# Four transfers for the key weight rows, two of them on ScalarE's queue, and a first tile scaled in halves

## The chip, the cores and the metric

The kernel runs on one core of one Trainium2 chip. The metric is device time in microseconds (us) of one execution; smaller is better. Before the change, three runs took 563.38, 563.44 and 564.0 us; their median is 563.44.

## The reference, cut to what matters

```python
xn = layernorm(x)                                  # x: 2048 x 512
q, k, v = split(xn @ wqkv)                         # 32 heads of 16
pq, pk = q @ w_phi, k @ w_phi                      # per head, 16 x 16
phi = concat(softmax(p), softmax(-p))              # for p = pq and p = pk
kv, z = phi_k^T v, sum(phi_k)                      # per head
s = ((phi_q kv) / (phi_q z + 1e-6)) @ wo
g = silu((relu(xn @ W_gate) * (xn @ W_up)) @ W_down)
out = x + s * g
```

All inputs are float32. Each large product is made of three products of float32r operands, a high and a low part (`mm3`, line 198).

## The kernel before

The 2048 rows of x are 16 tiles of 128 rows. For each tile n the kernel normalizes the rows, transposes the tile on TensorE (`transpose_x`, line 297), and projects it to keys and values (`project`, line 358), and later to queries. The gate, up and down products follow, for 11 chunks f of 128 hidden columns, and last the output product. TensorE has work in every stage.

The key and query weights are not used as they come. `fold(w, raw, k)` (line 243) multiplies row block k of the transposed weight with a block-diagonal matrix made of `w_phi` (the tile `cb`): four float32 products of 128x128 into one PSUM bank, each recorded as two passes. ScalarE and VectorE then split the result into high and low parts (`split`, line 193; tiles `wkh` and `wkl`). So the folds of the key weight need `cb` and the rows of `wkT`; the first key product `pk` needs the folds and the transposed first tile.

What happens first, by the program (lines 950 to 1018):

- Lines 953 to 966 issue loads, nearly all on SP's queue: x tile 0; the identity (`ident`) on ScalarE's queue; `cb`; row blocks 0 and 1 of `wkT` in one transfer of 512 KB; row block 2; row block 3 (256 KB each); x tile 1; then query rows, value rows and more x tiles.
- Lines 968 to 972: VectorE clears a tile `idle`, and TensorE multiplies it with itself twelve times (24 passes, `pidle`). Nothing reads these products. Line 973 fills `mhalf`, the exponent -0.5 that the norm needs.
- Lines 983 to 993: `norm_vector(0)` (line 278) takes mean and variance on VectorE and the power on GpSimd; `norm_vector_apply(0)` (line 288) scales the tile in one VectorE instruction; `turn(0, False)` (line 319) transposes it in four 128x128 steps and copies the high part to `XT`. Then come the folds of row blocks 0 and 1, then of 2 and 3.
- Line 995: `pk`, the first key product, then the folds of the query weight, and for the value weight the high parts on ScalarE (`wv_hi`) and the low parts on GpSimd (`wv_lo`, tile `wvl`).
- The value product of tile 0, `pv`, reads `wvl`.

The order of each engine's instructions is the order in which the program writes them: every call goes through `InOrder` (line 45). For later stages the program decides when to write a piece of side work by a planner, `Clock` (line 62). It adds up an estimate for each engine, takes 8000 of its units for a DMA to land (line 69), and lets a piece of work go when its inputs are due (`due`, line 121). `pump` (line 134) is called between products.

The weights of the hidden chunks f = 2 and f = 3 (`AHEAD`, line 36) are loaded first, during the early tiles, by `f_load` (line 455): for each f two transfers of 256 KB into the halves of one tile `rawg` and one into `rawd`. `all_preps` (line 1020) then waits 30 steps of 512 planner units before `f_prep` uses them.

Of the kernel before, what the change touches and what calls it, by code (L numbers as in the profile page):

```python
# [9 lines left out]
AF = mybir.ActivationFunctionType  # L10
ALU = mybir.AluOpType
AX = mybir.AxisListType

P = 128
S = 2048
D = 512
# [3 lines left out]
KD = D // P  # L20
# [15 lines left out]
AHEAD = (2, 3)  # L36
# [122 lines left out]
def layer_kernel(ctx: ExitStack, tc: tile.TileContext, x, wkT, wqT, wv, wo, wf, cst, out):  # L159
    pace = Clock()  # L160
    nc = InOrder(tc, pace)
# [4 lines left out]
    def ps(shape=(P, 512), name="ps"):  # L166
        return pp.tile(list(shape), F32, tag="ps", name=name)

    def u8(shape, name, dt=F32):
        return sb.tile(list(shape), dt, tag="u8", bufs=B8, name=name)  # L170

    def u4(shape, name, dt=F32):
        return sb.tile(list(shape), dt, tag="u4", bufs=B4, name=name)

    def u2(shape, name, dt=F32):
        return sb.tile(list(shape), dt, tag="u2", bufs=B2, name=name)

    def small(n, name, bufs=3):
        return sb.tile([P, n], F32, tag=name, bufs=bufs, name=name)
# [43 lines left out]
    def load_x(n):  # L223
        b, i = order[n]
        t = b * TPB + i
        X[n] = u2((P, D), "xt")
        nc.sync.dma_start(X[n], x[t * P:(t + 1) * P, :])
# [26 lines left out]
    mhalf = sb.tile([P, 96], F32, name="mhalf")[:, 0:1]  # L254
# [32 lines left out]

    def norm_vector_apply(n):
        xn, xt, mv, rs = XN[n]
        nc.vector.tensor_scalar(xn, xt, mv[:, 0:1], rs, op0=ALU.subtract, op1=ALU.mult)  # L290
        XN[n] = xn

    def cols(n):
# [151 lines left out]
    RAW, FT, WD = {}, {}, {}  # L445

    def two(name, apart):
        if apart:
            return [u2((P, 2, 2, P), name) for c in range(2)]
        t = u4((P, 2, 2, 2, P), name)  # L450
        return [t[:, c] for c in range(2)]
# [1 line left out]
    DONE = set()  # L453

    def f_load(f):
        RAW[f] = two("rawg", f not in AHEAD), u2((P, D), "rawd")
        for c in range(2):
            nc.sync.dma_start(RAW[f][0][c].rearrange("p k s f -> p (k s f)"), wf[f][:, c * 512:(c + 1) * 512])
        nc.sync.dma_start(RAW[f][1], wf[f][:, 1024:])

    def w_pair(name):
# [10 lines left out]
    def f_prep(f, keep=True):  # L472
# [47 lines left out]
        if keep:  # L520
            FT[f], WD[f] = [wa, wb, wc, wd], fd
            nxt = f + 1
            while nxt in AHEAD:
                nxt += 1
            del rg, rd, ta, tb
            if nxt < NF:
                f_load(nxt)
# [422 lines left out]
    wk_raw, wv_raw, wq_raw = u8((P, KD, D), "wkT"), u8((P, KD, D), "wvr"), u8((P, KD, D), "wqT")  # L950
    bd_sb = u2((P, KD, P), "cb")
    ident = sb.tile([P, P], F32, name="ident")
    load_x(0)
    nc.scalar.dma_start(ident, cst[:, KD, :])
    nc.sync.dma_start(bd_sb, cst[:, :KD, :])
    nc.sync.dma_start(wk_raw[:, 0:2, :], wkT[:, 0:2, :])
    nc.sync.dma_start(wk_raw[:, 2, :], wkT[:, 2, :])
    nc.sync.dma_start(wk_raw[:, 3, :], wkT[:, 3, :])
    load_x(1)
    nc.sync.dma_start(wq_raw[:, 0:2, :], wqT[:, 0:2, :])  # L960
    nc.sync.dma_start(wv_raw[:, 0:2, :], wv[:, 0:2, :])
# [3 lines left out]
    for n in range(3, 7):  # L965
        load_x(n)

    idle = u2((P, P), "idle")
    nc.vector.memset(idle, 0.0)
    p = ps((P, P), name="pidle")  # L970
    for _ in range(12):
        nc.tensor.matmul(p, idle, idle, start=True, stop=True)
    nc.vector.memset(mhalf, -0.5)
    zacc = u4((P, H, 2, DH), "zacc")

    WK, WV, WQ = w_tile("wk"), w_tile("wv"), w_tile("wq")
# [4 lines left out]
    def wv_lo(k):  # L981
        add(nc.gpsimd, by_parity(WV[k][1]), even_first(wv_raw[:, k, :]), f32(by_parity(WV[k][0])), ALU.subtract)
    norm_vector(0)
    norm_vector_apply(0)
    px = turn(0, False)
    folds = [fold(WK, wk_raw[:, k, :], k) for k in range(2)]
# [5 lines left out]
    norm_vector(1)  # L992
    folds[1]()
    norm_vector_apply(1)
    pk = project(0, WK, "pk")
    folds = [fold(WQ, wq_raw[:, k, :], k) for k in range(2)]
# [14 lines left out]
    for s in range(2):  # L1011
        exp_part(early, s)
    norm_vector(3)
    norm_vector_apply(2)
    sums_x(1)
    folds[0]()
# [3 lines left out]
    def all_preps():  # L1020
        for f in AHEAD:
            f_load(f)
            yield 30,
            yield from f_prep(f, False)
        f_load(0)
        yield 30,
        for f in range(NF):
            if f not in AHEAD:
                while at[0] < (START[f] if f < 2 else N + f - 1):
                    yield 3,  # L1030
                if f in WO_WITH:
                    wo_fetch(WO_WITH.index(f))
                yield from f_prep(f)
                if f in WO_WITH:
                    yield from wo_prep(WO_WITH.index(f))
# [289 lines left out]
```

## Time and profile before

| quantity | value |
|---|---|
| median of three runs | 563.44 us |
| profiled execution, own time | 564.6 us |
| its span, from the first to the last instruction | 562.8 us |
| mean granted TensorE clock in the span | 0.998 |
| TensorE products busy | 555.9 us, 99% |
| VectorE, ScalarE, GpSimd busy | 412.4, 282.3, 416.7 us |
| DMA | 137.98 MB, mean 245 GB/s |

The profile is of one execution. The own time of that execution holds 1.8 us beside its span. In rows of a timeline the columns are start, duration (both us), engine, source line, operation, the tile written, the tiles read, the shapes and the count; in brackets stands how long the engine was idle before it and what released it. Nearly all rows have line 58, since all instructions go through one helper, so one goes by the names of tiles. PE is TensorE's products, PEld its weight loads, DVE VectorE, ACT ScalarE, POOL GpSimd, SP the SyncE queue; ACTq and SPq are the issues of DMAs. A row of waits gives the waiting engine and its tile, what it waited for, the us in total, how many times, and the longest. Consecutive products overlap in the records.

### The profile page before, as it was taken

The numbers are of one execution on the slowest core, as the hardware profiler recorded it, in microseconds if no ns is written. First come the engines' busy times: TensorE is split into PE (matmuls) and PEld (weight loads), VectorE is DVE, ScalarE is ACT, GpSimd is POOL, SyncE is SP. The second block draws the span as 40 slices with busy tenths as digits, with TensorE's granted clock in tenths as the row PEclk, the third lists the DMA queues.
The fourth block names the chain that finished last, engine by engine and source line by source line (L and its number), as shares of the span: only waits on it lengthen the run. The fifth ranks groups of instructions, "written<-read, shape, count | busy, mean of one in ns | idle before, by whom it ended". The sixth has DMA issues, their size and how long they took to land.

```text
span 562.8 us, 8204 instructions
## 1 busy us (share of the span) xinstructions
PE 555.9 (99%) x2620; PEld 465.1 (83%) x2620; DVE 412.4 (73%) x621; ACT 282.3 (50%) x504; POOL 416.7 (74%) x356
## 2 busy tenths in 40 slices
PE   8999999999999999999999999999999999999996
PEld 7888888888888888888888888888888888888885
DVE  4978866677656898999797432799995959684224
ACT  3898787675555446444425251234563644535500
POOL 1689987999888386998889242573779888888375
PEclk9999999999999999999999999999999999999999
DMA  8349999856599828979867999997485766669684
GB/s 294 122 137 257 260 278 292 243 162 188 149 295 314 325 77 278 321 276 315 289 219 230 252 364 418 397 380 272 119 244 169 219 192 206 206 200 263 165 236 183
DMA packets 84538, 137.98 MB, mean 245 GB/s; under 512 B 7824, under 2 KB 34320, under 8 KB 83600
## 3 DMA queue, kind: packets, MB, share of 16 engines
q1 hardware_dynamic: 81040, 125.33, 65.4%
q0 software_dynamic: 3312, 12.06, 11.1%
q8 instruction: 21, 0.34, 0.2%
q14 instruction: 21, 0.17, 0.1%
q10 hardware_dynamic: 144, 0.07, 0.0%
HBM read 76.87 MB, written 52.69 MB: 230 GB/s over the span
## 4 chain that ended last, share of the span: by engine, by line
PE 97%; DMA 1%; DVE 1%; issue 0%; SPq 0%; DVEq 0%
PE py L58 21%; PE pc L58 11%; PE pd L58 11%; PE pa L58 11%; PE pv L58 8%; PE pk L58 8%; PE pq L58 8%; PE pso L58 7%; PE pb L58 5%; PE pkv L58 3%; PE pnum L58 3%; PE pfold L58 1%; PE pxT L58 1%; DMA wkT<-wkT 1%; DVE yk L58 1%
## 5 line engine op out<-in xcount | busy, mean ns | idle before, releaser
L58 PE MATMUL py<-fdh,hh 128*128 128x512 f32 x176 | 68.5, 389 | 0.0
L58 PE MATMUL py<-fdh,hl 128*128 128x512 f32 x176 | 68.5, 389 | 0.0
L58 PE MATMUL py<-fdl,hh 128*128 128x512 f32 x176 | 68.5, 389 | 0.0
L58 PE MATMUL pa<-XT,wa 128*128 128x512 f32 x264 | 67.3, 389 | 0.0
L58 POOL TENSOR_TENSOR hl<-e,hh 128x512 fp32r<-128x512 f32 x22 | 28.5, 1295 | 45.4 <-ACT hh L58 40.4
L58 PEld LDWEIGHTS pa<-XT,wa 128*128 128x128 f32 x264 | 49.5, 188 | 10.2
L58 ACT ACTIVATE hh<-e 128x512 fp32r<-128x512 f32 x22 | 13.9, 633 | 73.1 <-DVE e L58 70.6
L58 DVE TENSOR_TENSOR y<-py,y 128x512 f32<-128x512 f32 x40 | 27.5, 689 | 24.7 <-PE py L58 24.6
L58 PE MATMUL pv<-wvh,XT 128*128 128x512 f32 x128 | 43.5, 401 | 0.0
L58 POOL TENSOR_TENSOR phl<-ek,phl 128x1024 fp32r<-128x1024 f32 x15 | 36.1, 2406 | 9.9 <-ACT phl L58 9.9
L58 PE MATMUL pk<-wkh,XT 128*128 128x512 f32 x128 | 42.4, 392 | 0.0
L58 POOL TENSOR_TENSOR hl<-u,hh 128x512 fp32r<-128x512 f32 x22 | 28.8, 1308 | 17.2 <-ACT hh L58 14.2
L58 POOL TENSOR_TENSOR ez<-eq,zB 128x1024 f32<-128x1024 f32 x16 | 38.7, 2424 | 3.3 <-ACT eq L58 2.7
L58 PE MATMUL pq<-XT,wqh 128*128 128x512 f32 (+1 forms) x144 | 40.3, 366 | 0.0
L58 PEld LDWEIGHTS py<-fdh,hl 128*128 128x128 f32 x176 | 33.0, 188 | 7.0
L58 PEld LDWEIGHTS py<-fdh,hh 128*128 128x128 f32 x176 | 33.0, 188 | 6.9
L58 PEld LDWEIGHTS py<-fdl,hh 128*128 128x128 f32 x176 | 33.0, 188 | 6.8
L58 POOL TENSOR_TENSOR ol<-of,oh 128x512 fp32r<-128x512 f32 (+1 forms) x13 | 19.9, 1552 | 24.2 <-ACT oh L58 15.3
L58 PE MATMUL pc<-XT,wc 128*128 128x512 f32 x132 | 34.9, 392 | 0.0
L58 PE MATMUL pd<-XT,wc 128*128 128x512 f32 x132 | 33.8, 389 | 0.0
L58 PE MATMUL pc<-XT,wb 128*128 128x512 f32 x132 | 33.7, 389 | 0.0
L58 PE MATMUL pd<-XT,wd 128*128 128x512 f32 x132 | 33.5, 389 | 0.0
(161 smaller groups left out, 1580.9 us busy)
## 6 DMA issues: line engine op xcount, KB each, us to landing
zacc<-ek POOLq DMA_DIRECT2D x15, 512.0 KB, 5.8
xts<-XT SPq DMA_DIRECT2D x4, 1792.0 KB
XT<-xts SPq DMA_DIRECT2D x7, 1024.0 KB, 19.6
wa<-ws SPq DMA_DIRECT2D x26, 256.0 KB, 5.4
wb<-ws SPq DMA_DIRECT2D x26, 256.0 KB, 4.3
wc<-ws SPq DMA_DIRECT2D x26, 256.0 KB, 5.1
rawg<-wf SPq DMA_DIRECT2D x22, 256.0 KB, 3.4
ws<-wa SPq DMA_DIRECT2D x22, 256.0 KB, 4.4
```

The source lines that it names most:

```text
L58: return self.tc.keep_in_program_order(op(*a, **k))
```

## The change

- The rows of `wkT` come in four transfers of 256 KB, one for each row block. Blocks 0 and 1 stay on SP's queue, behind `cb`. Blocks 2 and 3 are issued on ScalarE's queue. Ahead of them in ScalarE's order stands a copy of one column out of the PSUM bank into which TensorE's first four idle products go, so ScalarE issues them after those products.
- Of the idle products there are eleven instead of twelve, four before that copy and seven in a second PSUM bank. The clearing of `idle` and the filling of `mhalf` stand ahead of the loads in the program.
- The first x tile is scaled in two VectorE instructions of 256 columns instead of one of 512. All others stay as they are.
- For f = 3 (`AHEAD[-1]`), the two gate and up transfers of 256 KB become one of 512 KB into the same tile.

```diff
     def norm_vector_apply(n):
         xn, xt, mv, rs = XN[n]
-        nc.vector.tensor_scalar(xn, xt, mv[:, 0:1], rs, op0=ALU.subtract, op1=ALU.mult)
+        for c in [slice(0, 256), slice(256, D)] if n == 0 else [slice(0, D)]:
+            nc.vector.tensor_scalar(xn[:, c], xt[:, c], mv[:, 0:1], rs, op0=ALU.subtract, op1=ALU.mult)
         XN[n] = xn
...
     def f_load(f):
-        RAW[f] = two("rawg", f not in AHEAD), u2((P, D), "rawd")
-        for c in range(2):
-            nc.sync.dma_start(RAW[f][0][c].rearrange("p k s f -> p (k s f)"), wf[f][:, c * 512:(c + 1) * 512])
+        if f == AHEAD[-1]:
+            t = u4((P, 2, 2, 2, P), "rawg")
+            RAW[f] = [t[:, c] for c in range(2)], u2((P, D), "rawd")
+            nc.sync.dma_start(t.rearrange("p c k s f -> p (c k s f)"), wf[f][:, :1024])
+        else:
+            RAW[f] = two("rawg", f not in AHEAD), u2((P, D), "rawd")
+            for c in range(2):
+                nc.sync.dma_start(RAW[f][0][c].rearrange("p k s f -> p (k s f)"), wf[f][:, c * 512:(c + 1) * 512])
         nc.sync.dma_start(RAW[f][1], wf[f][:, 1024:])
...
+    idle = u2((P, P), "idle")
+    nc.vector.memset(idle, 0.0)
+    nc.vector.memset(mhalf, -0.5)
     load_x(0)
     nc.scalar.dma_start(ident, cst[:, KD, :])
     nc.sync.dma_start(bd_sb, cst[:, :KD, :])
-    nc.sync.dma_start(wk_raw[:, 0:2, :], wkT[:, 0:2, :])
-    nc.sync.dma_start(wk_raw[:, 2, :], wkT[:, 2, :])
-    nc.sync.dma_start(wk_raw[:, 3, :], wkT[:, 3, :])
+    for k in range(2):
+        nc.sync.dma_start(wk_raw[:, k, :], wkT[:, k, :])
+
+    p = ps((P, P), name="pidle")
+    for _ in range(4):
+        nc.tensor.matmul(p, idle, idle, start=True, stop=True)
+    nc.scalar.activation(small(1, "lm"), p[:, 0:1], AF.Copy)
+    for k in range(2, KD):
+        nc.scalar.dma_start(wk_raw[:, k, :], wkT[:, k, :])
     load_x(1)
...
-    idle = u2((P, P), "idle")
-    nc.vector.memset(idle, 0.0)
     p = ps((P, P), name="pidle")
-    for _ in range(12):
+    for _ in range(7):
         nc.tensor.matmul(p, idle, idle, start=True, stop=True)
-    nc.vector.memset(mhalf, -0.5)
```

## The prediction, made before the change was run

> **What bounds the kernel now.** I read the page first, then the waits of PE, the chain of waits over the first 40 us, and the timeline of the first 21 us.
>
> ```profile
> span 562.8 us, 8204 instructions
> PE 555.9 (99%) x2620; PEld 465.1 (83%) x2620; DVE 412.4 (73%) x621; ACT 282.3 (50%) x504; POOL 416.7 (74%) x356
> ...
> PE 97%; DMA 1%; DVE 1%; issue 0%; SPq 0%; DVEq 0%
> ```
>
> TensorE is busy for 99% of the span, and the chain that ended last is 97% TensorE. So time is saved by fewer products or fewer holes between them. The waits of PE over the whole span are only three:
>
> ```profile
> PE pidle L58 <- DVE mhalf L58: 1.1, 1, 1.1
> PE pfold L58 <- DMA wkT<-wkT: 0.6, 1, 0.6
> PE pxT L58 <- DVE xn L58: 0.4, 1, 0.4
> ```
>
> All three lie in the first 7.3 us. From there PE never waits, until its last product, so whatever PE gains before that point reaches the end of the kernel, unless a wait that is hidden today comes out. The chain of the start:
>
> ```profile
> 1.66 5.51 DMA wkT<-wkT
> 7.16 0.14 issue
> 7.30 3.81 PE pfold L58 x32
> ```
>
> The 512 KB transfer of key weight rows 0 and 1 (wk01) is issued at 1.66 us and lands at 7.17; the folds start 0.14 later. The parallel chain ends at the transposes of the first tile (start, duration, engine):
>
> ```profile
> 3.69 0.70 DVE L58 BATCH_NORM_STATS2 bs<-xt 128x6 f32<-128x512 f32 x1 [2.67 <-DMA xt<-x]
> ...
> 4.63 0.15 DVE L58 TENSOR_SCALAR br<-bm 128x1 f32<-128x1 f32 x1
> ...
> 5.47 0.55 DVE L58 TENSOR_SCALAR xn<-xt,bm,br 128x512 f32<-128x512 f32 x1 [0.68 <-POOL br L58]
> ...
> 6.07 0.66 PE L58 MATMUL pxT<-ident,xn 128*128 128x128 f32 x4 [0.41 <-DVE xn L58]
> 6.77 0.60 ACT L58 ACTIVATE XT<-pxT 128x512 fp32r<-128x512 f32 x1 [4.31 <-PE pxT L58]
> ```
>
> The four transposes end at 6.73. PE starts a successor before the modelled end, as a later pair shows:
>
> ```profile
> 15.58 0.60 PE L58 MATMUL pxT<-ident,xn 128*128 128x128 f32 x4
> 16.01 1.95 PE L58 MATMUL pfold<-cb,wqT 128*128 128x128 f32 x16
> ```
>
> There 15.58 + 0.60 = 16.18 and the fold starts at 16.01, 0.17 sooner. So the folds could start at 6.73 - 0.17 = 6.56, and start at 7.30: 0.74 us wait for wk01 alone.
>
> **The change, part by part.** *Row transfers.* Who issues what, and when a landing let go of an issue on SP:
>
> ```profile
> 0.74 0.40 ACTq L58 DMA_DIRECT2D ident<-cst  x1
> 0.75 0.39 SPq L58 DMA_DIRECT2D xt<-x  x1
> ...
> 1.19 0.42 SPq L58 DMA_DIRECT2D cb<-cst  x1
> 1.66 1.37 SPq L58 DMA_DIRECT2D wkT<-wkT  x3
> 3.07 0.44 SPq L58 DMA_DIRECT2D xt<-x  x1
> ```
> ```profile
> 7.18 0.33 SPq L58 DMA_DIRECT2D wvr<-wv  x1
> 7.83 0.33 SPq L58 DMA_DIRECT2D xt<-x  x1
> 8.67 0.98 SPq L58 DMA_DIRECT2D xt<-x  x2
> ```
> ```profile
> SPq L58 <- DMA wkT<-wkT: 1.4, 3, 0.6
> ```
>
> Three SP issues waited for the landings of the three wkT transfers, so these landed at about 7.17, 7.82 and 8.66: row 2 only 0.65 us after the pair, row 3 0.84 after that. Landing times from the issue, for the two small neighbours and the pair:
>
> ```profile
> cb<-cst SPq DMA_DIRECT2D x1, 256.0 KB, 3.1
> ident<-cst ACTq DMA_DIRECT2D x1, 64.0 KB, 3.1
> wkT<-wkT SPq DMA_DIRECT2D x1, 512.0 KB, 5.5
> ```
>
> So cb lands at 1.19 + 3.1 = 4.3, and the 512 KB of rows 0 and 1 take 2.87 us more. Row 0 as its own transfer (wk0) lands between 4.3 + 0.65 = 4.95 (the quickest 256 KB step) and 7.17 (it carries less than the pair that landed there, with the same ahead of it); I take half of the 2.87: 5.74.
>
> Rows 2 and 3 go to ACT's queue behind a copy that waits for four products. Rows of the idle products and of ACT's first work:
>
> ```profile
> 1.06 4.61 PE L58 MATMUL pidle<-idle 128*128 128x128 f32 x24 [1.06 <-DVE mhalf L58]
> 1.18 1.28 ACT L58 ACT_TABLE_LOAD   x1 [1.18 <-PEq L1317]
> ```
> ```profile
> L58 ACT ACTIVATE ones<-one 128x128 fp32r<-128x128 f32 x1 | 0.3, 289 | 0.0
> ```
>
> Twelve products are 24 passes in 4.61 us, 0.19 each, somewhat slower at first; four products (8 passes) end at about 2.7 to 3.0. The copy, at most the 0.29 of the row above, ends near 3.3. The table load (to 2.46) is done by then, so the copy adds no load of its own. The issues take 0.4 each: row 2 at about 3.3, row 3 at 3.7, where SP issues them at about 2.1 and 2.6 now. Behind the waiting copy on ACT are only these two issues and then the XT copy of 6.77; who waits for them are the folds of rows 2 and 3. SP is rid of one issue in all, and x tile 1, the query and the value rows can come 0.47 us sooner on it. The wait of the twelfth issue on the fourth one's landing (7.17) suggests that an issue waits for the landing eight before it; the first query rows would then be ninth and wait for x or ident (3.7 to 3.84) instead of going at 3.56. The queue still holds row 1 and tile 1 then, so nothing is lost.
>
> Row 1 is the disputed price. The folds want it at fold start + 8 passes. A pass is 0.11: in the folds of wkT, 32 passes run from 7.30 to 10.83, where the last starts.
>
> ```profile
> 10.83 0.28 PE L58 MATMUL pfold<-cb,wkT 128*128 128x128 f32 x1
> 10.86 0.47 PE L58 MATMUL pk<-wkh,XT 128*128 128x512 f32 x1
> ```
>
> The landing's lower end is 5.74 + 0.65 = 6.4. Its upper end is 8.66, when all four rows are in today, if rows 2 and 3 share the engines with it evenly. ACT's transfers start over a us later than SP's row 1, so I take the landing of the same bytes today plus half of one 256 KB step: 7.17 + 0.33 = 7.50.
>
> The Trainium skill, "DMA: Bandwidth & Descriptors", section "Issuing engines are not separate DMA queues", says that transfers from scalar, sync and gpsimd run on the same 16 engines and interleave, so a second issuing engine only saves issue time. Its section "Queues, rings and completion order" has each engine serve its queues in turn, packet by packet. This speaks against the change; the trace agrees so far that ident (64 KB, ACT) and the first x tile (256 KB, SP), issued together, landed within 0.2 us of each other (0.74 + 3.1 = 3.84, and 3.69 at the latest, when its first reader started). By the section on queues the sum would be that of the rival with even shares, below.
>
> *The halves.* One 128x512 scaling takes 0.55 and a 128x1 one 0.15; between them in proportion, a half of 256 columns takes 0.35. The second half ends at 5.47 + 0.70 = 6.17, not 6.02, but the first two transposes run meanwhile. The third starts at 6.22 (0.05 of handing on, as 6.02 to 6.07), two steps of some 0.12 later the folds can start: 6.47, against 6.56. Ends: at half of 0.55 per half, 6.32; at 0.55 each, 6.87.
>
> *Idle products.* Eleven for twelve: two passes of 0.11 less at their end, so they end near 5.45 instead of 5.67, while the first transpose comes at 5.47 + 0.35 + 0.05 = 5.87 instead of 6.07. The hole stays 0.4. Cost nothing; the cover is the norm of tile 0. The memsets move ahead in the program, but are already DVE's first work; nothing.
>
> *One transfer for the gate rows of f = 3.* One issue of about 0.4 us less on SP.
>
> ```profile
> rawg<-wf SPq DMA_DIRECT2D x22, 256.0 KB, 3.4
> ```
>
> A 512 KB landing instead of two of 256 KB may come one 0.65 step later. The planner lets 30 x 512 columns of PE's clock pass between this load and its first use, some 15 us against the 3.4 above; cost nothing, and if the cover were gone, the price is 0.65 on GpSimd, not on PE. The planner's own clock starts one product earlier and sees two DVE instructions for one; its due times are relative, so I take the order of everything later as unchanged.
>
> **The sum.** Row 0 (5.74 + 0.14) is in before 6.47; row 1 is wanted at 6.47 + 0.88 = 7.35 and lets the fold start at 7.50 + 0.14 = 7.64. Today that fold starts at 7.30 + 0.88 = 8.18. Gain 0.54 us. Rows 2 and 3 are wanted at 8.52 and 9.40; their landings of today, 7.82 and 8.66, would do, so the copy on ACT is hidden by 0.7.
>
> What is late next: the value rows.
>
> ```profile
> wvr<-wv SPq DMA_DIRECT2D x1, 512.0 KB, 8.6
> ```
> ```profile
> 15.78 0.60 ACT L58 ACTIVATE wqh<-pfold 128x512 fp32r<-128x512 f32 x1 [0.30 <-PE pfold L58]
> 16.27 1.14 ACT L58 ACTIVATE wvh<-wvr 128x512 fp32r<-128x512 f32 x2
> ```
> ```profile
> 16.97 2.55 POOL L58 TENSOR_TENSOR wvl<-wvr,wvh 128x512 fp32r<-128x512 f32 x2 [1.08 <-ACT wvh L58]
> ```
> ```profile
> 20.12 0.39 PE L58 MATMUL pv<-wvl,XT 128*128 128x512 f32 x1
> ```
>
> Value rows 2 and 3 land at 7.18 + 8.6 = 15.78, bound by the bytes ahead of them; ACT takes them at 16.27, GpSimd ends their low part at 19.52, and PE wants it at 20.12. With PE 0.54 earlier, ACT would take them at 15.73, so it waits 0.05 to 0.15; the low part then ends near 19.1 and is wanted at 19.58. Hidden, by 0.4.
>
> The profiled execution took 564.6 us, 1.8 beside its span of 562.8. Minus 0.54: span 562.26, execution 564.06. The runs shown have a median of 563.44, 1.16 under the profiled one; minus 0.54 that is **562.9 us**.
>
> **The rivals.** *Row 1 is hidden too.* For it: its bytes have the same SP queue ahead as the pair that landed at 7.17, and it is needed in by 7.35 - 0.14 = 7.21. Against it: two transfers come beside it. Gain 8.18 - 7.35 = 0.83, time 562.6 (562.46 with the quicker halves).
>
> *Even shares make row 1 late* (the other side). Place: the fold of row 1. If ACT's rows take every second packet, rows 1 and 3 come in together, when all four are in: 8.66. The fold starts at 8.80 instead of 8.18: 0.62 slower, 564.06. It decides from a landing of row 1 after 8.18 - 0.14 = 8.04. For it: ident beside x. Against it: ACT's rows start later and row 0 is partly through by then. If tile 1's 256 KB got in between as well (0.65 more), 1.27 slower, 564.7.
>
> *The gain is handed back at pv.* If value rows 2 and 3 land one 0.65 step later, at 16.43, ACT takes them at 16.5 and the low part ends 3.25 later, 19.75; with 0.1 of handing on that is 0.27 after PE's wish of 19.58: 563.17. For it: the margin is 0.4. Against it: the bytes ahead of them are the same.
>
> *The change does not do what it says*: ACT's copy or the second half are late, or the planner orders later work otherwise; no row prices this, and I give it both signs.
>
> **How the numbers follow.** Forecast (part of the gain, wk1 between 7.21 and 8.04) 0.45; hidden 0.25; even shares 0.14; handed back 0.10; the rest 0.06. Below 562.31 or above 564.57 is over 0.2%, about what a measurement of this kernel can tell from no change. Faster by that needs more than the 0.83 to 0.98 of the best case: 0.07. Slower by that needs tile 1 in between or the unpriced rest: 0.06. Within: 0.87. The range reaches from just under the hidden case, 562.3, to just over even shares, 564.2.
>
> **What would show it.** The changed profile should have the first transpose near 5.87, the folds starting near 6.47 and no PE wait for xn of more than 0.45; a PE wait for wkT of about 0.3 ahead of the fold of row 1, none ahead of rows 2 and 3; pk starting about 0.54 sooner than at 10.86; and no wait of PE from there on. Wrong would be: the first fold still waiting for wkT until past 7 us (row 0 not quicker alone), the fold of row 1 after 8.18 (even shares), ACT's issues after 4 us, or a PE wait for wvl near 19.6.

## The result, and the profile after

The changed kernel took 567.89 us (median of 6 runs, 566.52 to 569.0), the kernel before on the same chip 563.25 (562.64 to 564.0). The ratio is 1.0072, with a 95% interval of 1.0052 to 1.0092: slower by some 4 us. The prediction was 562.9 with a range up to 564.2; it was wrong. The six times fall into two groups, 566.52 to 567.19 at a granted clock of 0.999 or 1.0 and 568.59 to 569.0 at 0.997, with the median in the gap between them; two experiments below, `copy_pad` and `shift1024`, have one execution each at a clock of 0.66 and 0.75, which their medians leave out and whose profiles are not used.

The page of the changed kernel, its span and its engines, and then the waits of PE over the whole span (us in total, times, longest):

```profile
span 564.7 us, 8205 instructions
...
PE 558.6 (99%) x2618; PEld 466.4 (83%) x2618; DVE 412.7 (73%) x622; ACT 282.7 (50%) x505; POOL 416.0 (74%) x356
```
```profile
PE pfold L58 <- DMA wkT<-wkT: 1.5, 2, 0.8
PE pidle L58 <- DVE mhalf L58: 1.1, 1, 1.1
```

Two waits for key weight rows stand where one stood, and PE is busy 2.7 us longer although it runs two passes fewer. The chain of waits over the first 40 us begins with a transfer that has nothing to do with the folds:

```profile
0.74 3.16 DMA ident<-cst
...
3.93 7.69 DMA wkT<-wkT
...
11.66 1.16 PE pfold L58 x8
```

Row 3 is issued at 3.93, held until `ident` has landed at 3.90, and lands at 11.62, where 8.66 had been counted on. The timeline of the changed kernel shows the same from the issuers' and from PE's side:

```profile
2.60 0.43 SPq L58 DMA_DIRECT2D xt<-x  x1
3.07 0.44 SPq L58 DMA_DIRECT2D wqT<-wqT  x1
3.18 0.17 ACT L58 ACTIVATE lm<-pidle 128x1 f32<-128x1 f32 x1 [0.71 <-PE pidle L58]
3.18 1.08 ACTq L58 DMA_DIRECT2D wkT<-wkT  x2
3.74 0.33 SPq L58 DMA_DIRECT2D wvr<-wv  x1
...
5.99 1.12 PE L58 MATMUL pxT<-ident,xn 128*128 128x128 f32 x4
...
6.90 2.08 PE L58 MATMUL pfold<-cb,wkT 128*128 128x128 f32 x16
...
7.35 0.33 SPq L58 DMA_DIRECT2D wvr<-wv  x1
...
8.56 3.92 SPq L58 DMA_DIRECT2D xt<-x  x5
...
9.71 1.16 PE L58 MATMUL pfold<-cb,wkT 128*128 128x128 f32 x8 [0.74 <-DMA wkT<-wkT]
...
11.66 1.16 PE L58 MATMUL pfold<-cb,wkT 128*128 128x128 f32 x8 [0.79 <-DMA wkT<-wkT]
...
12.58 0.48 PE L58 MATMUL pk<-wkh,XT 128*128 128x512 f32 x1
```

The first sixteen passes run through: row 1 has landed by 7.34 (it lets the value load on SP go at 7.35), x tile 1 by 8.55 (so do the next x loads at 8.56). Rows 2 and 3 let PE go at 9.71 and 11.66. `pk` starts at 12.58 instead of 10.86, so 1.7 us are lost at the start.

The medians lie 4.6 apart, the two profiled spans only 1.9. PE's busy time in windows shows why (stretch, its length, PE busy and count, clock, DMA share, GB/s), first of the kernel before, then of the changed one:

```profile
0.00:13.00 13.00, 10.96 (x69) 1.00 0.84 285
13.00:167.00 154.00, 154.00 (x803) 1.00 0.75 216
167.00:550.00 383.00, 383.00 (x1706) 1.00 0.78 258
550.00:570.00 20.00, 7.89 (x47) 0.90 0.28 105
```
```profile
0.00:13.00 13.00, 10.41 (x60) 1.00 0.87 304
13.00:167.00 154.00, 154.00 (x805) 1.00 0.74 211
167.00:550.00 383.00, 383.00 (x1698) 1.00 0.79 258
550.00:570.00 20.00, 11.22 (x60) 0.92 0.39 139
```

In the two middle stretches PE is busy without a gap in both. In the last stretch PE of the kernel before is idle for 562.8 - 550 - 7.89 = 4.9 us, of the changed one for 564.7 - 550 - 11.22 = 3.5: the profiled execution of before has an end 1.4 longer (its own time, 564.6, is 1.3 above its median here; that of after, 566.5, is 1.4 below). In the profiles of the experiments below at full clock the same idle time is 3.5 to 3.8 where some tiles lie 32 to 128 bytes further on (see below) and 3.5 to 4.8 in the others; whether the 1.4 is chance is not shown. So the start loses 1.7, the end gives 1.4 back, and 1.9 - 1.7 + 1.4 = 1.6 are lost between, where PE never waits. There the products themselves are slower. Groups by line and form (busy us, mean ns of one), before and then after:

```profile
L58 PE MATMUL py<-fdh,hh 128*128 128x512 f32 x176 | 68.5, 389 | 0.0
...
L58 PE MATMUL pso<-woh,oh 128*128 128x512 f32 x60 | 23.3, 389 | 0.0
```
```profile
L58 PE MATMUL py<-fdh,hh 128*128 128x512 f32 x176 | 68.6, 390 | 0.0
...
L58 PE MATMUL pso<-woh,oh 128*128 128x512 f32 x60 | 23.8, 396 | 0.0
```

The same instructions on the same shapes take 7 ns more in `pso` (and 2 to 8 in `pnum`, of which there are 48), while `py` stays. With three `pso` groups of 60 that is 180 x 7 ns = 1.3 us, and some 0.2 for `pnum`.

### The profile page after: what moved, and what is told of

Same layout as the page of the kernel before. It is cut to its first block, busy times and chain, and to the rows that moved or that the text cites. A ratio compares the mean times of both kernels' runs of the same rounds, so it can differ in the third digit from the quotient of the medians.

```text
span 564.7 us, 8205 instructions
## 1 busy us (share of the span) xinstructions
PE 558.6 (99%) x2618; PEld 466.4 (83%) x2618; DVE 412.7 (73%) x622; ACT 282.7 (50%) x505; POOL 416.0 (74%) x356
## 4 chain that ended last, share of the span: by engine, by line
PE 97%; DMA 2%; DVE 0%; issue 0%
PE py L58 21%; PE pc L58 11%; PE pd L58 11%; PE pa L58 11%; PE pso L58 8%; PE pv L58 8%; PE pk L58 8%; PE pq L58 8%; PE pb L58 5%; PE pnum L58 3%; PE pkv L58 3%; DMA wkT<-wkT 1%; PE pxT L58 1%; PE pfold L58 1%; DMA ident<-cst 1%; PE pz L58 0%
```

## The theories

**For the late rows.** *A*: ACT's queue takes turns with SP's, and rows 2 and 3 are slow because SP's query and value rows run beside them. *O*: transfers land nearly in the order in which they are issued, whichever queue issues them; rows 2 and 3 are late because by 3.18 and 3.93 x tile 1, query and value rows have been issued ahead of them. By O the order is to blame, not the queue.

**For the slower products.** *P*: the copy's output is the first use of a small tile `lm` (three buffers of 32 bytes). In the compiled programs these lie at 191488, where the first of eight tiles of the kind `u4` lay before (no view of the profile shows an address); all eight move up by 96 bytes. `oh`, `ol`, `pTh`, `pTl` and the `z` tiles are `u4`; `hh`, the operand of `py`, is not and keeps its kind of address. The rival is *C*: the holes at the start, or what they do to PE's clock, cost time beyond their own length and later on.

## The experiments

Times are medians; each ratio is against the kernel before, run beside it (its median was 563.50 to 563.63 us).

**Rows 2 and 3 on SP behind the others, the copy kept** (`sp_rows`, against the changed kernel):

```diff
     nc.scalar.activation(small(1, "lm"), p[:, 0:1], AF.Copy)
     for k in range(2, KD):
-        nc.scalar.dma_start(wk_raw[:, k, :], wkT[:, k, :])
+        nc.sync.dma_start(wk_raw[:, k, :], wkT[:, k, :])
```

> The changed kernel, but key weight rows 2 and 3 are issued on SP's queue right behind rows 0 and 1 (the copy on ACT stays, nothing waits for it). Theory A (shared turns: on ACT's queue the rows take turns with the x, query and value loads of SP's queue and so land at 9.67 and 11.62): with the rows ahead of those loads they land near 7.9 and 8.7, PE waits for wkT no more than 0.2 us in all, and the time is 562.5 to 563.4, at or under before (563.25). Theory C (half of the 4.6 us is TensorE's clock, which the two holes of 0.7 to 0.8 us send to half speed in some executions): the spread of 2.5 us goes with the holes, granted clock 0.998 or more. Theory D (something later, by the shifted transfers or the order of ACT's work): the time stays above 565.

Measured: 564.65, ratio 1.0022 (1.0012 to 1.0032). PE waits for no row of the key weight, and `pk` starts at 10.73. Of some 4 us, 2.8 are gone, but it is not level with the kernel before: `pso` is slow here too.

```profile
L58 PE MATMUL pso<-woh,oh 128*128 128x512 f32 x60 | 23.8, 396 | 0.0
```

**ACT's rows without the copy ahead** (`act_no_copy`):

```diff
-    nc.scalar.activation(small(1, "lm"), p[:, 0:1], AF.Copy)
```

> The changed kernel without the one-column copy on ACT, so that rows 2 and 3 go on ACT's queue at about 1.2 and 1.6 us instead of 3.2 and 3.9. Theory B (the late issue is the fault, not the queue): they land by 8.7, PE does not wait for them, time 562.5 to 563.5. Theory A (shared turns): they start to move with x tile 0 and delay it and rows 0 and 1 by 0.3 to 0.8 us, but land themselves at about 6.5 to 8.5; the holes of PE ahead of rows 2 and 3 go, the first transposes come later; time 563 to 564.5.

Measured: 564.96, ratio 1.0026 (1.0007 to 1.0044). ACT now issues row 2 at 1.18 and row 3 at 1.66, so now row 0, on SP, is the late one. The chain of waits:

```profile
1.65 5.91 DMA wkT<-wkT
...
7.70 3.81 PE pfold L58 x32
```

Row 0 lands at 7.56 instead of about 6; the folds start at 7.70 and then run through. The queue is the same as in the changed kernel, only the time of issue differs, and rows 2 and 3 are no longer late. Both theories expected that, and a delay of row 0 is what A expected (0.3 to 0.8 us; it was some 1.5), so this run doesn't decide between them. `pso` is back at 389 ns, with `lm` no longer in front. The time is above both expectations: `pk` starts at 11.26, 0.4 later than before, and the other microsecond of the loss is not explained here.

**Query and value rows behind rows 2 and 3 on ACT** (`act_first`), which takes SP's competing loads away as A has them:

```diff
-    nc.sync.dma_start(wq_raw[:, 0:2, :], wqT[:, 0:2, :])
-    nc.sync.dma_start(wv_raw[:, 0:2, :], wv[:, 0:2, :])
-    nc.sync.dma_start(wq_raw[:, 2:4, :], wqT[:, 2:4, :])
+    nc.scalar.dma_start(wq_raw[:, 0:2, :], wqT[:, 0:2, :])
+    nc.scalar.dma_start(wv_raw[:, 0:2, :], wv[:, 0:2, :])
+    nc.scalar.dma_start(wq_raw[:, 2:4, :], wqT[:, 2:4, :])
     load_x(2)
-    nc.sync.dma_start(wv_raw[:, 2:4, :], wv[:, 2:4, :])
+    nc.scalar.dma_start(wv_raw[:, 2:4, :], wv[:, 2:4, :])
```

> The changed kernel with the four query and value loads moved from SP's queue to ACT's, behind rows 2 and 3. The rows are issued as late as in the changed kernel (3.2 to 3.9) on the same queue, but share turns only with rows 0 and 1 and x tiles. Theory A (shared turns with 2 MB of query and value rows): rows 2 and 3 land near 7.5 and 8.7, PE waits under 0.3 us for them, time about 563 to 564. Theory B (late issue): they land as in the changed kernel, at 9.7 and 11.6, PE waits 1.5 us, time 566 to 568.

Measured: 568.18, ratio 1.0084 (1.0070 to 1.0098). The timeline:

```profile
2.59 8.81 SPq L58 DMA_DIRECT2D xt<-x  x7
...
9.85 1.16 PE L58 MATMUL pfold<-cb,wkT 128*128 128x128 f32 x8 [0.61 <-DMA wkT<-wkT]
...
11.36 1.16 PE L58 MATMUL pfold<-cb,wkT 128*128 128x128 f32 x8 [0.35 <-DMA wkT<-wkT]
11.72 0.60 ACT L58 ACTIVATE XT<-pxT 128x512 fp32r<-128x512 f32 x1 [8.38 <-DMA wqT<-wqT]
```

With those loads out of SP's way, rows 2 and 3 still come in at 9.8 and 11.3: x tiles 1 to 3 have moved up on SP into their place. The DMA view from 3.7 to 3.8 us shows the issue of tile 3 and its time to landing:

```profile
xt<-x SPq DMA_DIRECT2D x1, 256.0 KB, 7.3
```

So it landed at about 11.0, between the two rows. A, as put, falls: the query and value rows as such are not to blame. That ACT's queue takes turns with whatever SP has in flight does not fall with it. Nor is a plain count of the bytes ahead enough for O: ahead of row 3 stood 768 KB of x here, against 256 KB of x and 1 MB of query and value rows in the changed kernel, and it landed only 0.3 sooner. The run also shows what ACT pays for loads: its copy of `XT` waits to 11.72 behind an issue that is itself waiting, and PE behind that.

**The halves alone** (`halves`, against the kernel before):

```diff
-        nc.vector.tensor_scalar(xn, xt, mv[:, 0:1], rs, op0=ALU.subtract, op1=ALU.mult)
+        for c in [slice(0, 256), slice(256, D)] if n == 0 else [slice(0, D)]:
+            nc.vector.tensor_scalar(xn[:, c], xt[:, c], mv[:, 0:1], rs, op0=ALU.subtract, op1=ALU.mult)
```

> The kernel before with the first tile scaled in two halves, nothing else. The folds wait for rows 0 and 1 until 7.3 in any case, so all theories expect no change: 563.0 to 563.5, first transpose at about 5.9 instead of 6.07, PE wait for wkT 0.1 to 0.2 longer. If halves alone cost over 0.5 us, they are a part of the loss.

Measured: 563.77, ratio 1.0002 (0.9990 to 1.0014). No difference that can be told. In its profiled execution PE had no wait for `xn` and the fold started at 6.62, with no wait for the pair of rows 0 and 1 either, which is one transfer here as before. The issue of the value load that waits for the pair's landing shows how far this varies between executions, all with the same first loads: it went at 7.18 in the kernel before, at 6.50 here and at 8.09 in `shift256` below.

**The copy without the shift** (`copy_pad`, and once more as `copy_pad2`; the copy writes into a spare column of the tile that holds `mhalf`, so the `u4` tiles stay where they were before):

```diff
-    mhalf = sb.tile([P, 96], F32, name="mhalf")[:, 0:1]
+    spare = sb.tile([P, 96], F32, name="mhalf")
+    mhalf = spare[:, 0:1]
...
-    nc.scalar.activation(small(1, "lm"), p[:, 0:1], AF.Copy)
+    nc.scalar.activation(spare[:, 64:65], p[:, 0:1], AF.Copy)
```

> The changed kernel, but the one-column copy on ACT writes into unused columns behind mhalf instead of into a new tile of the tag lm. Theory P (placement: with lm first used there, the eight 4 KB tiles of the tag u4, which hold pT, oh, ol, z and the like, lie 96 bytes further on, and every product that reads them takes 0.234 us a step instead of 0.227): they lie where they did before, pso steps are 0.227 again, and the time is 1.3 to 1.9 us under the changed kernel: 566.0 to 566.6, with rows 2 and 3 still late (PE waits for wkT 1.2 to 1.8 us). Rival Q (the steps of pso depend on when things run, not on the place): pso steps 0.234, time 567.5 to 568.5.

> The program of copy_pad once more, for a profile at the full clock. Theory P: pso steps 0.227, PE waits for wkT 1.2 to 1.8 us, median 566.0 to 566.6.

Measured: 565.88, ratio 1.0045 (1.0026 to 1.0063), and 565.73, ratio 1.0038 (1.0023 to 1.0052). Waits of PE and the `pso` group of `copy_pad2`:

```profile
PE pfold L58 <- DMA wkT<-wkT: 2.6, 2, 1.8
```
```profile
L58 PE MATMUL pso<-woh,oh 128*128 128x512 f32 x60 | 23.3, 389 | 0.0
```

The late rows are all there, row 3 landed at 12.61 in this execution, and the products are as quick as before. So the late rows alone cost 2.1 to 2.5 us.

**The shift without anything else** (`shift_only`, against the kernel before):

```diff
     ident = sb.tile([P, P], F32, name="ident")
+    nc.vector.memset(small(1, "lm"), 0.0)
     load_x(0)
```

> The kernel before, with the tag lm first used ahead of all loads (one column of it cleared by VectorE), nothing else. Theory P (placement): the u4 tiles lie 96 bytes further on, pso steps are 0.234, time 1.3 to 1.9 us over before: 564.8 to 565.4. Rival Q: no change, 563.2 to 563.8, pso steps 0.227.

Measured: 565.14, ratio 1.0022 (1.0006 to 1.0038), with `pso` at 396 ns. No transfer and no copy is changed, and 1.2 us (by the ratio) to 1.6 us (by the medians) are lost. In its profiled execution the pair also came late and `pk` started at 11.64; since its first loads are those of before, the times of ten executions weigh more here than that one start.

**An earlier copy** (`copy_early`: `copy_pad` with the copy behind one idle product instead of four, and ten after it instead of seven), by which O wants rows 2 and 3 sooner:

```diff
-    for _ in range(4):
+    for _ in range(1):
...
-    for _ in range(7):
+    for _ in range(10):
```

> As copy_pad, but the copy waits for one idle product instead of four (and ten follow instead of seven), so rows 2 and 3 go on ACT's queue at about 2.3 and 2.7 us, between row 1 (2.1) and most of x tile 1 and the query rows (2.6, 3.1) of SP's queue. Theory O (order of issue: transfers land in the order in which they are issued, over both queues): rows 2 and 3 land near 8.3 and 9.3 instead of 9.67 and 11.62, PE waits for wkT 0.5 us at most, time 563 to 564. Theory A (turns between the queues, packet by packet): issuing 0.9 us sooner moves the landings by about 0.5 us only, PE still waits about 1 us, time 565 to 566.

Measured: 564.17, ratio 1.0012 (1.0001 to 1.0023). The timeline shows the issues of ACT and SP, and the folds:

```profile
1.65 0.90 SPq L58 DMA_DIRECT2D wkT<-wkT  x2
1.90 0.82 ACTq L58 DMA_DIRECT2D wkT<-wkT  x2
...
7.14 1.13 PE L58 MATMUL pfold<-cb,wkT 128*128 128x128 f32 x8 [0.17 <-DMA wkT<-wkT]
...
8.83 1.38 PE L58 MATMUL pfold<-cb,wkT 128*128 128x128 f32 x10 [0.56 <-DMA wkT<-wkT]
```

Row 2, issued between rows 0 and 1, now goes ahead of row 1: row 1 is in at 8.79 (7.34 in the changed kernel), and row 0 at about 7.0, so neighbours share. From 5 to 6 and from 6 to 7 us SP's queue moved 63 and 74 packets and ACT's 63 and 73. After that PE doesn't wait for rows 2 and 3. Moving the issue by 1.3 us moved row 2 from 9.7 to before 8.8. The time is a little above O's range and well below A's; the 0.7 us that PE still waits are for rows 0 and 1. So the time of issue decides whether rows 2 and 3 are late, as O has it, while the two queues take turns once both are moving, as A has it.

**All four rows on SP, no copy** (`sp_no_copy`):

```diff
-    nc.scalar.activation(small(1, "lm"), p[:, 0:1], AF.Copy)
     for k in range(2, KD):
-        nc.scalar.dma_start(wk_raw[:, k, :], wkT[:, k, :])
+        nc.sync.dma_start(wk_raw[:, k, :], wkT[:, k, :])
```

> The changed kernel with all four rows on SP's queue and without the copy: what is left of the change are the four transfers, the halves, eleven idle products and the joined gate transfer of f = 3. Theories P and O together: pso steps 0.227, PE waits for wkT under 0.3 us, time 562.5 to 563.4, at or just under before. If it stays at the 564.65 of sp_rows, the placement is not what made sp_rows slower.

Measured: 563.0, ratio 0.9993 (0.9982 to 1.0003), the lowest of all here, though not told from no change. Its timeline:

```profile
1.65 1.85 SPq L58 DMA_DIRECT2D wkT<-wkT  x4
...
6.65 3.56 PE L58 MATMUL pfold<-cb,wkT 128*128 128x128 f32 x29
```

The folds run through from 6.65. PE has no wait left but the first one, for `mhalf`. The four kernels make a table of two causes, which add up:

| ratio to before | `u4` tiles 96 bytes up | `u4` tiles in place |
|---|---|---|
| rows 2, 3 on ACT behind the copy | 1.0072 (the change) | 1.0045, 1.0038 (`copy_pad`, `copy_pad2`) |
| rows 2, 3 on SP | 1.0022 (`sp_rows`) | 0.9993 (`sp_no_copy`) |

Down a column, the queue and the copy ahead of it, which set the time of issue, cost 0.0050 and 0.0045 to 0.0052 (2.5 to 2.9 us); along a row, the shift costs 0.0027 to 0.0034 and 0.0029 (1.5 to 1.9 us). The intervals are 0.002 to 0.004 wide, so the second figures are rough.

**Is it the address?** (`shift32`, `shift64`, `shift128`, `shift256`, `shift1024`: the kernel before with one small tile of so many bytes a partition in front, cleared once; here 32)

```diff
+    nc.vector.memset(small(8, "pad", 1), 0.0)
```

> The kernel before, with a tile of 32 bytes placed ahead of the u4 tiles (VectorE clears it at the start), so that these and all that lies behind them move by 32 bytes instead of 96. If what counts is a 64-byte boundary (191488 is one, 191584 and 191520 are not), pso steps are 0.234 and the time is 1.2 to 1.8 us over before. If only some larger shift counts, pso steps are 0.227 and the time is that of before.

> As shift32 with 64 bytes. If a 64-byte boundary is what counts, pso steps stay 0.227 and the time is that of before, 563.0 to 564.0. If a larger one counts (128 or more), pso steps are 0.234 and the time 1.2 to 1.8 us over before.

> The kernel before with a tile of 128 bytes, cleared by VectorE, ahead of the u4 tiles, which move from 191488 to 191616. If what counts is the address against a boundary of 128 bytes or less: pso products at 389 ns as in the kernel before and a time within 0.15% of it (562.8 to 564.5). If the boundary is wider, or the extra tile or instruction itself is what costs: 394 to 396 ns and 564.5 to 565.2.

> The same with 256 bytes. Address against a boundary of 256 or less: 389 ns and the time of before (562.8 to 564.5). A wider boundary, or the extra tile or instruction: 394 to 396 ns and 564.5 to 565.2.

> The same with 1024 bytes, by which all remainders of the u4 addresses up to 1024 stay as before. If the address is what costs: 389 ns and the time of before (562.8 to 564.5). If the extra tile or its instruction costs, wherever the u4 tiles then lie: 394 to 396 ns and 564.5 to 565.2.

Measured: 565.17, ratio 1.0032 (1.0019 to 1.0045); 564.5, 1.0015 (1.0002 to 1.0027); 564.61, 1.0030 (1.0018 to 1.0041); 563.93, 1.0003 (0.9988 to 1.0018); 563.15, 0.9994 (0.9981 to 1.0007). The `pso` group of `shift128` and of `shift256`:

```profile
L58 PE MATMUL pso<-woh,oh 128*128 128x512 f32 x60 | 23.7, 395 | 0.0
```
```profile
L58 PE MATMUL pso<-woh,oh 128*128 128x512 f32 x60 | 23.3, 389 | 0.0
```

The tile and its instruction are there in all five. The loss is there with 32, 64 and 128 bytes (0.9 to 1.5 us), and with 256 and 1024 none can be told. 191488 is 748 x 256. So it is the address: in this kernel `pso` products of 128x512 whose `u4` operands begin 32, 64, 96 or 128 bytes past a multiple of 256 take 6 to 7 ns more than 389. Those of 128x256 do not: 282 to 283 ns before, 280 to 281 in the changed kernel. Other tiles that lie behind the `u4` tiles move as well; that the `u4` operands are what counts rests on `pso`, `pnum` and `pz` reading them, and on `py`, which doesn't, staying.

**The holes filled** (`fill`: the changed kernel with four idle products ahead of each fold of rows 2 and 3), for C, which expects PE to lose less without holes:

```diff
-    folds = [fold(WK, wk_raw[:, k, :], k) for k in range(2, KD)]
+    folds = []
+    for k in range(2, KD):
+        p = ps((P, P), name="pidle")
+        for _ in range(4):
+            nc.tensor.matmul(p, idle, idle, start=True, stop=True)
+        folds.append(fold(WK, wk_raw[:, k, :], k))
```

> The changed kernel with four more idle products ahead of the fold of row 2 and four ahead of that of row 3, so that TensorE works through most of the two holes. Theory C (the slower half of the changed kernel's executions, 568.6 to 569.0 against 566.5 to 567.2, lost 1.7 us to TensorE's clock, halved for some 3.4 us after the holes): no execution over 567.5, median 566.4 to 567.0, spread about 1 us. Rival (the spread comes from the transfers or from when the clock first rises): spread still 2 us or more, median 567.5 to 568.5.

Measured: 568.07, ratio 1.0073 (1.0057 to 1.0089): no gain. The chain of waits:

```profile
3.18 7.49 DMA wkT<-wkT
...
10.71 1.16 PE pfold L58 x8
11.87 0.89 PE pidle L58 x8
12.76 1.09 PE pfold L58 x8
```

Row 2 landed at 10.67 here, a microsecond later than in the profile of the changed kernel (9.67); so much does it vary between executions. The second four idle products also run ahead of the fold of row 3, and `pk` starts at 13.61 instead of 12.58. So `fill` cannot refute C. Its median is what the rival expected, but its spread is what C expected: 0.8 us over five executions at a clock of 0.998 to 1.0, where the changed kernel has 2.5 over six. Between the executions of the changed kernel and of the kernel before at a clock of 0.999 or 1.0 alone, the medians are 567.04 and 563.3 to 563.6, some 3.6 apart, about the sum of the late rows and the address. The rest of the 4.6, about 1 us, goes with the three executions at 0.997, of which no profile was kept. Against C as their cause stands `act_first`, whose five executions have holes of 0.2 to 0.7 us and a clock of 1.0. What brings them stays open.

## Why the prediction was wrong, step by step

- **The step that failed**: "Rows 2 and 3 are wanted at 8.52 and 9.40; their landings of today, 7.82 and 8.66, would do, so the copy on ACT is hidden by 0.7." The issue times (3.3 and 3.7 forecast, 3.18 and 3.93 measured) were nearly right. But the landings of today belong to issues at 2.1 and 2.6, ahead of x tile 1. Moved 1.1 to 1.3 us later, the rows fell behind 256 KB of x and among 1 MB of query and value rows. They landed at 9.67 and 11.62 in the profile, 1.9 and 3.0 us later than before, and PE waited 0.74 and 0.79 for them. The prediction had the right rule in hand: it called the landing of the value rows "bound by the bytes ahead of them", and didn't apply it to rows 2 and 3. Price: 2.1 to 2.9 us by `copy_pad`, `copy_pad2` and the table.
- **Not in the prediction at all**: the new output tile of the copy, and with it the addresses of the `u4` tiles. Price: 1.2 to 1.9 us by the table and `shift_only`. "The change does not do what it says" was the only case that left room for it, at 0.06 and without a price. The sum of the two, 3.3 to 4.8, covers the 4.1 of the ratio and the 4.6 between the medians.
- **The wait that was to go**: the landing of rows 0 and 1 at 7.17 was read from one execution. With the same first loads, the issue that waits for it went at 6.50 in `halves` and at 8.09 in `shift256`, and PE's wait for it ran from nothing in the one to 1.57 us in the other. So the 0.74 us on which the forecast gain rests was one draw from a wide spread, not a property of the kernel.
- **Row 1**: forecast 7.50 with a wait of PE; it landed at 7.34 and PE didn't wait. The rival "row 1 is hidden too" was right on this point. "Even shares" was not: rows 1 and 3 landed 4.3 us apart. This bears on the rule of the Trainium skill weighed there ("DMA: Bandwidth & Descriptors", section "Queues, rings and completion order": each engine serves its queues in turn). The rows of the transfers in flight, by queue, for 4 to 5, 5 to 6, 6 to 7 and 8 to 9 us of the changed kernel (packets, MB, share; q1 carries SP's loads, q10 ACT's):

```profile
q1 hardware_dynamic: 146, 0.27, 106.9%
```
```profile
q1 hardware_dynamic: 130, 0.24, 75.5%
q10 hardware_dynamic: 14, 0.03, 7.3%
```
```profile
q1 hardware_dynamic: 119, 0.25, 73.9%
q10 hardware_dynamic: 52, 0.10, 26.4%
```
```profile
q1 hardware_dynamic: 78, 0.28, 70.6%
q10 hardware_dynamic: 67, 0.12, 31.0%
```

  Row 2 was issued at 3.18, and from 4 to 5 us no packet of ACT's queue is recorded; then 14 beside 130, and 52 beside 119. Had the queues been served in turn from the issue on, half of the packets would have been its own. From 8 us on that is nearly so: 67 beside 78, then 74 beside 77 from 9 to 10. So the rule agrees with the trace once both queues move, and what the rival "even shares" had wrong is the start: the first packet of row 2 moved at about 5.5, some 2.3 us after its issue. Whether it waited there for the bytes issued before it, on whichever queue, is not shown. What the Trainium skill says on that page under "Issuing engines are not separate DMA queues", that a second issuer only saves time of issue, agrees: SP issued two rows fewer and its first query rows at 3.07 instead of 3.56, and nothing was gained.
- **The halves**: forecast 0.35 each and a first transpose at 5.87; two took 0.74, and the transposes began at 5.99. Right in size. That the idle products cost nothing was wrong in size: 22 passes ended at 6.12, where 24 ended at 5.67 before, and the first transposes took 1.12 instead of 0.66. So the folds started at 6.90, not 6.47. The granted clock reads 1.00 over these 13 us in both profiles; in `act_first` the same 22 passes took 4.21. Why they vary stays open.
- **Value rows at `pv`, the merged gate transfer, the order of later work**: PE has no wait after the folds; nothing was handed back there. Right. That PE's early loss reaches the end was right too: it did, with the sign turned round.
- **The gain that was forecast**, 0.54, fits what is left when rows 2 and 3 stay on SP and no tile is moved: `sp_no_copy` has 563.0 beside 563.55. But its interval holds no change as well, and so the gain is not shown.

## What to carry to other kernels

A transfer that is issued later competes anew with all that has been issued on any queue by then: count those bytes for a first estimate, and never carry over its old landing time. Read a landing from several executions before you price a wait on it. A new small tile can move the addresses of tiles that the change doesn't touch; when untouched products change their mean duration by a few ns, compare the addresses of their operands first, and put scratch outputs where nothing moves. And before two profiles are subtracted, see how far each execution lies from its median: here 2.7 of the 4.6 us between the medians didn't show in the difference of the spans.

## What was not expected of the hardware

- Transfers of SP's and ACT's queues landed nearly in the order of their issue: on the changed kernel, issues at 2.12 (SP), 2.60 (SP), 3.18 (ACT) and 3.93 (ACT) landed at 7.34, 8.55, 9.67 and 11.62. The first packet of the one issued at 3.18 moved at about 5.5; from 8 to 10 us the two queues moved 67 beside 78 and 74 beside 77 packets. In `copy_early`, where row 2 was issued 0.2 us ahead of row 1 on the other queue, row 1 landed at 8.79.
- The `pso` products of float32r operands of 128x512 took 389 ns with the `u4` operand at a multiple of 256 bytes and 395 to 396 with 32, 64, 96 or 128 bytes more; offsets between 128 and 256 weren't tried. Which of an instruction's reads pays for it wasn't tried.
- The second issue on ACT waited for a landing eight transfers back over both queues (`ident`, 3.90), as SP's had in the profile before. Whether the program's own semaphores ask for this or the queues do is not shown.
